# The experts' stage of an attention-and-experts kernel: the order of its operations taken from a written list instead of from a greedy planner

## The chip, the cores and the metric

One core of a Trainium2 chip runs the whole program. The metric is the device time of one execution in microseconds (us), the median of three runs. The core's engines are TensorE (PE, with its weight loads on PEld), VectorE (DVE), ScalarE (ACT), GpSimd (POOL) and the queue SP that only issues transfers. Every engine works through its own instructions strictly in the order of the program and meets the others through semaphores.

## What is computed

The reference first does attention with pooled queries for 64 heads (sequence 1152, head size 64, queries pooled by two) and lays the result out as 4608 tokens of 512 values. Then each token goes to one of eight experts. Tokens are taken greedily by their gate value, and each expert takes 576:

```
logits = x @ w_gate                      # 4608 x 8
for idx in argsort(-logits.flatten()):   # the largest value of all first
    tok, e = idx // 8, idx % 8
    if tok is free and expert e has room: give tok to e
for e in range(8):
    out[tokens of e] = relu(x[tokens of e] @ w1[e]) @ w2[e]    # 512 -> 1024 -> 512
```

## The kernel before

Attention comes first and isn't touched. It leaves the tokens in DRAM (`x_dram`) and the gate values in `L`. The stage that the change touches is `experts` (L1092). It handles the experts one after the other, k = 0 to 7, in the order in which they fill up, and each of them has three parts:

- `route(k)` (L1245) finds the k-th expert and its 576 tokens. For k = 0 to 6 it makes eight rounds: DVE compares keys (`cmp`, L1278), PE counts (`pc`, five small products, L1284), DVE sums its own part (`own`, L1287 and L1289), PE makes the total (`pt`, L1293), DVE narrows the search (`fa`, `fl`). Then come the members (`cl`, `me`), a running sum (`px`, L1362 and L1365), offsets on PE (`pf`, L1370 to L1373), a table lookup on PE (`pl`, L1418), the token numbers on DVE (`ix`, L1422 to L1429), and what is left for the next expert (`tk`, L1466 and L1468; `p9` on PE, L1470; `lf`, `se`). Products `p9`, `pc` and `pt` and what `ix` reads lie in one PSUM tile, `rt`.
- `fetch(k)` (L1555) issues, on POOL's software DMA queue, the load of W1 (`dw`, in two halves for k = 0), the gathers of the tokens in five chunks of up to 128 rows (`dx`, L1564), and the load of W2 (`dv`, L1559). It turns the tokens over (by PE transposes for k below 2, by DVE and SP's queue after that) and splits tokens and weights into a high and a low part: ACT makes the high parts (`xh`, `wh`, `vh`), DVE or POOL the low ones (`xl`, `wl`, `vl`). For k = 0 the first quarter of W1's low part is DVE's (L1633), the rest POOL's (L1634).
- `ffn(k)` (L1639) makes the first layer: for each of 8 blocks of 128 features and each half of the tokens (256 and 320 columns) twelve products (`mm`, L1650), a relu on ACT (`re`, L1655), the low part of the result on DVE (`rs`, L1659 and L1662). Then it makes the second layer: five chunks of tokens, 24 products each or 16 for the last and smaller one (`m2`, L1680 and L1677), an output step on ACT (`ot`; chunk 4 also needs one on DVE, L1690), and a scatter to DRAM on POOL's queue (`pu`, L1697).

Nothing of that is run when it is written down. Each operation is given to `od.add` with its engine, an assumed duration, what it reads and writes, and a tag. `od.emit` (L80 and L1709) then fixes the order in which the program is made, and so the order on every engine. Before, `od` is an `Order` (L51): a greedy planner that follows a clock of assumed durations and, whenever an engine is free, takes of the ready operations the one with the best priority. The priority is the expert's place plus a lead for each tag (`ELEAD`, L1079); `ELATE` (L1085) and the waits in L43 to L48 correct the assumed times at which results are ready. Every single product is an operation of its own there. The small filler products of expert 0's routing (`warm`, L1256) have no tag.

Of the kernel before, what the change touches and what calls it, by code (L numbers as in the profile page):

```python
# [10 lines left out]
def _warn_once_fixed(msg, *args, **kwargs):  # L11
# [31 lines left out]
EOWN = {"PE": 0, "ACT": 140, "DVE": 120, "POOL": 130, "SP": 60}  # L43
EWAIT = {"PE": {"ACT": 205, "DVE": 205, "POOL": 205, "SP": 205},
         "ACT": {"PE": 190, "DVE": 145, "POOL": 170, "SP": 150},
         "DVE": {"PE": 180, "ACT": 130, "POOL": 160, "SP": 150},
         "POOL": {"PE": 130, "ACT": 110, "DVE": 110, "SP": 100},
         "SP": {"PE": 60, "ACT": 60, "DVE": 60, "POOL": 60}}  # L48


class Order:  # L51
# [10 lines left out]
    def __init__(self, lead={}, late={}):  # L62
        self.items, self.lead, self.late = [], lead, late
        self.of, self.cur, self.kind, self.stick, self.early, self.lock = [], None, [], 0, (), []
        self.switch = 83

    def add(self, t, eng, dur, fn, r=(), w=(), late=0, first=0, tag=None, kind=0, lock=None, k=None):

        if self.cur == 0 and tag in self.early:
            first = 1  # L70
        if self.cur == 0 and tag:
            tag = "0" + tag
        late = late + self.late.get(tag, 0)
        pri = t + self.lead.get(tag, 0) + (self.lead.get(f"{tag}.{k}", 0) if k is not None else 0)
        self.items.append((t, len(self.items), eng, dur, fn, tuple(r), tuple(w), late, (-first, pri)))
        self.of.append(self.cur)
        self.kind.append(kind)
        self.lock.append(eng == "POOL" if lock is None else lock)
# [84 lines left out]
class Timed(Order):  # L163
# [21 lines left out]
    def emit(self):  # L185
        items = sorted(range(len(self.items)), key=lambda i: (self.items[i][0], i))
        writer, readers, n = {}, {}, len(items)
        need = [set() for _ in range(n)]
        for i, j in enumerate(items):
            _, _, _, _, _, r, w, _, _ = self.items[j]  # L190
            for k in r:
                if k in writer:
                    need[i].add(writer[k])
                readers.setdefault(k, []).append(i)
            for k in w:
                if k in writer:
                    need[i].add(writer[k])
                need[i].update(readers.get(k, ()))
                readers[k] = []
                writer[k] = i  # L200
            need[i].discard(i)
        users, left = [[] for _ in range(n)], [len(x) for x in need]
        for i, x in enumerate(need):
            for j in x:
                users[j].append(i)
        heap = [(self.when(items[i]), i) for i in range(n) if not left[i]]
        heapq.heapify(heap)
        done = 0
        while heap:
            _, i = heapq.heappop(heap)  # L210
            self.items[items[i]][4]()
            done += 1
            for j in users[i]:
                left[j] -= 1
                if not left[j]:
                    heapq.heappush(heap, (self.when(items[j]), j))
        assert done == n


# [283 lines left out]
def attention(ctx, tc, top, kb, sx, kt, qt, v, wg, x_dram, L, npair=NPAIR):  # L503
# [549 lines left out]
    for n in range(1, npair, 2):  # L1053
# [8 lines left out]
        else:  # L1062
# [13 lines left out]

LT = {"dve": 0, "pe": 0, "x": 8000, "w": 9900, "w0": 3700, "w1": 8000, "x0": 3000, "zd": 0, "kd": 2, "cs": 4, "wn": 4,
      "xm": 7500, "xp": 4}
ELEAD = {"ar": 4.9, "be": 51.6, "bo": 2.8, "cl": 28.5, "cmp": 29.1, "dv": 1.5, "dw": -46.1, "dx": -41.8,  # L1079
# [5 lines left out]
ELATE = {"ar": -300, "bo": -300, "cl": -300, "cmp": 150, "dv": 1900, "dw": 750, "dx": 1500, "fa": -150, "fl": -300,  # L1085
# [4 lines left out]


def experts(ctx, tc, top, kb, sx, x_dram, L, w1, w2, out, C):  # L1092
    nc = tc.nc
    const = ctx.enter_context(tc.tile_pool(name="moe_const", bufs=1))
    psum = ctx.enter_context(tc.tile_pool(name="moe_psum", bufs=1, space=PSUM))
    od = Order(ELEAD, ELATE)
    od.OWN, od.WAIT, od.switch = EOWN, EWAIT, 125
    J = NBLK

    def one(shape, dt, name):  # L1100
# [65 lines left out]
    re = early([128, 1], F32, "re")  # L1166
# [22 lines left out]
    ws = [x.bitcast(F32)[:, 1:2] for x in we]  # L1189
# [12 lines left out]
    rb, tb = rt[:, :128], rt[:, 128:]  # L1202
# [560 lines left out]
```

## Time and profile before

| | us |
|---|---|
| median of 3 runs (1226.16 to 1227.74) | 1226.99 |
| time of the profiled execution | 1229.76 |
| its span, first to last instruction | 1227.9 |

The span is what the trace's clock counts. The execution's own time is 1.86 us more, and it is 2.77 us above the median of the three runs. In the trace the experts' first DVE instruction stands at 751.24 us and PE's last product ends at 1222.13 us. A view of stretches gives the busy time of each engine in it; a row of the timeline gives start, duration, engine, line and operation, and in brackets how long the engine had been idle before it and what released it.

### The profile page before, as it was taken

To read this page: it belongs to the slowest core of one execution; us is meant where nothing else is said; L and a number is where in the kernel's file an instruction comes from. 1 tells how busy PE (TensorE), PEld (TensorE's weight loads), DVE (VectorE), ACT (ScalarE), POOL (GpSimd) and SP (SyncE) were. 2 spreads that over 40 slices of the span, in tenths; PEclk is the share of its full clock that TensorE was granted. 3 is DMA by queue.
4 is the path that set the end of the run, shared out by engine and by line. 5 is a ranking of instruction groups with operands and counts; after the bars stand their busy time and mean duration, and the time that the engine had idled before them with its cause. 6 is when DMAs were issued, how large, how long until landed. Compare 5 with 4: busy or idle time off the path is not lost.

```text
span 1227.9 us, 37291 instructions
## 1 busy us (share of the span) xinstructions
PE 1171.8 (95%) x14875; PEld 806.2 (66%) x14875; DVE 977.8 (80%) x2327; ACT 868.1 (71%) x1603; POOL 897.7 (73%) x913
## 2 busy tenths in 40 slices
PE   7899999999899999999999997799999999999998
PEld 4566666666566666666666665567767777787876
DVE  7999999999999999999999955888988888442120
ACT  6788887987787987887879671376567564766831
POOL 4588888888788888888888882355677746769541
PEclk8899999999999999999999998999999999999999
DMA  8665665675565675666565310514544436345211
GB/s 212 147 172 133 176 168 129 158 182 124 145 176 121 166 179 132 162 169 151 144 177 143 82 48 21 176 35 167 189 153 149 162 124 214 86 168 167 88 40 39
DMA packets 95692, 171.07 MB, mean 139 GB/s; under 512 B 17694, under 2 KB 54558, under 8 KB 93342
## 3 DMA queue, kind: packets, MB, share of 16 engines
q1 hardware_dynamic: 82574, 107.09, 33.1%
q0 software_dynamic: 12800, 61.58, 17.0%
q8 instruction: 117, 1.92, 0.7%
q14 instruction: 57, 0.47, 0.1%
q10 hardware_dynamic: 144, 0.02, 0.0%
HBM read 99.63 MB, written 18.87 MB: 97 GB/s over the span
## 4 chain that ended last, share of the span: by engine, by line
PE 70%; DVE 18%; issue 5%; ACT 2%; DMA 2%; POOL 1%; SPq 0%; POOLq 0%; DVEq 0%; ACTq 0%
PE av L874 13%; PE po L1680 12%; PE ph L1650 12%; DVE MX L741 7%; PE sc L840 6%; PE sc L841 6%; PE mt L748 5%; PE kb L840 3%; PE kb L841 3%; PE av L910 3%; DVE PM L862 1%; PE mt L937 1%; PE rt L1284 1%; DVE V L691 1%; PE po L1677 1%
## 5 line engine op out<-in xcount | busy, mean ns | idle before, releaser
L862 POOL TENSOR_TENSOR PM<-P 128x512 f16<-128x512 f32 x537 | 586.5, 1160 | 116.4 <-ACT P L857 104.3
L741 DVE TENSOR_REDUCE MX<-mt 128x2 f32<-128x1024 f32 (+2 forms) x341 | 374.0, 1130 | 18.7 <-PE mt L748 13.1
L874 PEld LDWEIGHTS <-P 128*128 128x128 bf16 x4608 | 230.0, 98 | 60.0 <-issue 26.3
L857 ACT ACTIVATE P<-sc 128x512 f32<-128x512 f32 x384 | 224.8, 605 | 46.4 <-PE sc L841 41.6
L874 PE MATMUL av<-V,P 128*128 128x65 f16 (+1 forms) x4608 | 243.3, 193 | 0.1
L874 PE MATMUL av<-V,PM 128*128 128x65 f16 x2304 | 235.4, 195 | 0.2 <-POOL PM L862 0.2
L874 PEld LDWEIGHTS <-PM 128*128 128x128 f16 x2304 | 212.2, 97 | 0.5 <-POOL PM L862 0.4
L841 PE MATMUL sc<-QB,KB 66*128 66x64 f16 (+2 forms) x768 | 179.1, 288 | 0.0
L840 PE MATMUL sc<-QA,KA 128*128 128x512 f16 (+1 forms) x768 | 177.7, 288 | 0.8 <-ACT P L857 0.3
L1680 PE MATMUL po<-W2H,HX 128*128 128x512 f32 x512 | 165.7, 398 | 0.0
L857 ACT ACTIVATE P<-kb 128x512 f32<-128x512 f32 x192 | 115.2, 600 | 65.9 <-PE kb L841 63.6
L840 PEld LDWEIGHTS <-KA 128*128 128x128 f16 x1152 | 96.9, 99 | 80.9 <-issue 41.2
L1650 PE MATMUL ph<-Xh,W1h 128*128 128x320 f16 (+1 forms) x512 | 147.0, 287 | 1.5 <-ACT Xh L1512 1.5
L1650 PE MATMUL ph<-Xl,W1h 128*128 128x320 f16 (+1 forms) x512 | 146.8, 287 | 0.6 <-DVE Xl L1514 0.6
L1650 PE MATMUL ph<-Xh,W1l 128*128 128x320 f16 (+1 forms) x512 | 146.9, 287 | 0.0
L1659 DVE SCALAR_TENSOR_TENSOR HX<-ph,HX 128x256 fp32r<-128x256 f32 x128 | 53.3, 417 | 95.4 <-ACT HX L1655 95.2
L1680 PE MATMUL po<-W2L,HX 128*128 128x512 f32 (+1 forms) x320 | 127.4, 398 | 0.0
L841 PEld LDWEIGHTS <-KB 66*128 66x128 f16 (+1 forms) x1152 | 95.3, 98 | 37.5 <-issue 2.7
L1650 PEld LDWEIGHTS <-W1h 128*128 128x128 f16 x1024 | 98.0, 98 | 29.9 <-issue 5.2
L1655 ACT ACTIVATE HX<-ph 128x256 fp32r<-128x256 f32 (+1 forms) x128 | 52.1, 409 | 86.8 <-PE ph L1650 83.3
L1680 PEld LDWEIGHTS po<-W2H,HX 128*128 128x128 f32 x512 | 94.6, 188 | 18.9 <-issue 1.5
L1634 POOL TENSOR_TENSOR W1l<-W,W1h 128x512 f16<-128x512 f32 x62 | 71.6, 1165 | 35.6 <-ACT W1h L1628 30.8
(270 smaller groups left out, 2272.9 us busy)
## 6 DMA issues: line engine op xcount, KB each, us to landing
KD<-in_kt_dram SPq DMA_DIRECT2D x64, 288.0 KB
VD<-in_v_dram SPq DMA_DIRECT2D x32, 576.0 KB
QA<-QH SPq DMA_DIRECT2D x128, 72.0 KB
KA<-KH SPq DMA_DIRECT2D x64, 144.0 KB
KB<-KH SPq DMA_DIRECT2D x64, 144.0 KB
KA<-KL SPq DMA_DIRECT2D x64, 144.0 KB
x_dram<-X SPq DMA_DIRECT2D x16, 576.0 KB
QS<-in_qt_dram SPq DMA_DIRECT2D x31, 288.0 KB
```

Of the source, the lines that this page charges most:

```text
L741: od.add(t, "DVE", d, lambda: nc.vector.tensor_reduce(dst, src, axis=AX.X, op=OP.max), r=[f"m{m}"], w=w, tag="mr", k=z)
L748: nc.tensor.matmul(mt[s][:, y], pairs[b][s], KH[i][h, ks], start=True, stop=True)
L840: nc.tensor.matmul(c, KA[i][:, s, ks], QA[i][:, s, qs], start=first, stop=False, skip_group_check=True)
L841: nc.tensor.matmul(c, KB[i][:kr, s, ks], QB[i][:kr, s, qs], start=False, stop=last, skip_group_check=True)
L857: od.add(g + 0.1, "ACT", 480, lambda: nc.scalar.activation(p, c, AF.Exp, scale=1.0 / UNIT), r=[ck], w=[("P32", g % NP)], tag="exp", k=g % ...
L862: od.add(g + 0.2, en, dur, lock=1, fn=lambda: eng.tensor_tensor(pm, p, hi, op=OP.subtract), r=[("P32", g % NP)], w=[("PM", g % NM)], tag=" ...
L874: nc.tensor.matmul(out, w[:, qs], v, start=kb == 0 and j == 0 and y == 0, stop=kb == NKB - 1 and y == 2, skip_group_check=True)
L1634: eng.tensor_tensor(o, a, b, op=OP.subtract), r=[key] + sr + [(nm + "H", z, y)], w=[(nm + "L", z, y)], first=first, lock=1, tag="wl" if nm ...
L1650: nc.tensor.matmul(p, a[:, d, fs], b[:, d, qs], start=z == 0, stop=z == 11)
L1655: nc.scalar.activation(HH[:, f, qs], p, AF.Relu)
L1659: V.scalar_tensor_tensor(HL[:, f, 64 + 256 * hf:320 + 256 * hf], p[:, :256], 0.0, h[:, :256], op0=OP.max, op1=OP.subtract)
L1680: nc.tensor.matmul(o[:n], a[:, z, q0:q0 + n], b[:, z], start=z == 0 and y == 0, stop=z == 7, skip_group_check=True)
```

## The change

A new class `Listed` takes the place of `Order` in `experts`. It puts the operations of a tag of one expert together in the order in which they were added: four `mm` products make one group, two `m2` products make one, everything else stands alone. Each group has a name (expert, tag, running number; operations without a tag get the engine's name, so the fillers are `pe_`) and a number in the table `ETIME`, 2503 of them, given in ns from the start of the stage. `emit` makes the groups in the order of these numbers, except that a group waits its turn until all groups that it depends on are made. The durations, leads and late times are not used any more. No operation is added, removed or given to another engine; the operands are the same, and attention is the same.

```
+
+class Listed(Order):
+
+    def __init__(self, table):
+        Order.__init__(self)
+        self.table, self.names = table, []
+
+    def add(self, t, eng, dur, fn, r=(), w=(), late=0, first=0, tag=None, kind=0, lock=None, k=None):
+        Order.add(self, t, eng, dur, fn, r, w, late, first, tag, kind, lock, k)
+        self.names.append((int(t // 10), tag or {"PE": "pe", "DVE": "dv", "POOL": "po", "ACT": "ac", "SP": "sp"}[eng] + "_"))
+
+    def emit(self):
+        group, made, seen = {}, [], {}
+        for i in sorted(range(len(self.items)), key=lambda i: (self.items[i][0], i)):
+            k, tag = self.names[i]
+            z = seen[k, tag] = seen.get((k, tag), -1) + 1
+            name = f"{k}{tag}{z // {'mm': 4, 'm2': 2}.get(tag, 1)}"
+            if name not in group:
+                group[name] = len(made)
+                made.append((name, [], [], []))
+            _, fns, r, w = made[group[name]]
+            fns.append(self.items[i][4])
+            r.extend(x for x in self.items[i][5] if x not in r)
+            w.extend(x for x in self.items[i][6] if x not in w)
+        n, writer, readers = len(made), {}, {}
+        need = [set() for _ in range(n)]
+        for i, (_, _, r, w) in enumerate(made):
+            for k in r:
+                if k in writer:
+                    need[i].add(writer[k])
+                readers.setdefault(k, []).append(i)
+            for k in w:
+                if k in writer:
+                    need[i].add(writer[k])
+                need[i].update(readers.get(k, ()))
+                readers[k] = []
+                writer[k] = i
+            need[i].discard(i)
+        users, left = [[] for _ in range(n)], [len(x) for x in need]
+        for i, x in enumerate(need):
+            for j in x:
+                users[j].append(i)
+        heap = [(self.table[made[i][0]], i) for i in range(n) if not left[i]]
+        heapq.heapify(heap)
+        done = 0
+        while heap:
+            _, i = heapq.heappop(heap)
+            for fn in made[i][1]:
+                fn()
+            done += 1
+            for j in users[i]:
+                left[j] -= 1
+                if not left[j]:
+                    heapq.heappush(heap, (self.table[made[j][0]], j))
         assert done == n
...
-ELEAD = {"ar": 4.9, "be": 51.6, "bo": 2.8, "cl": 28.5, "cmp": 29.1, "dv": 1.5, "dw": -46.1, "dx": -41.8,
...
+ETIME = {"0be0": 0, "0be1": 580, "0be2": 1100, "0be3": 1620, "0ke0": 490, "0ke1": 950, "0ke2": 1470, "0ke3": 1990,
+         ...
+         "0ke8": 40973, "0ke9": 38213, "0po_0": 26276, "0dx0": 30168, "0dx1": 31468, "0dx2": 33186, "0dx3": 34582,
+         "0dx4": 35882, "0po_1": 37182, "0dv0": 40836, "0tr0": 34150, "0tr1": 34368, "0xh0": 34791, "0xl0": 35573,
+         ...
+         "0ws1": 34959, "0ws2": 48224, "0ws3": 48968, "0wi0": 40803, "0wi1": 49258, "0wh0": 35271, "0wl0": 36173,
+         "0wh1": 35786, "0wl1": 36863, "0wh2": 36781, "0wl2": 38282, "0wh3": 38341, "0wl3": 39591, "0wh4": 49268,
+         ...
+         "0vh0": 50526, "0vl0": 51776, "0vh1": 51606, "0vl1": 53021, "0vh2": 55796, "0vl2": 57094, "0vh3": 57956,
+         ...
+         75211, "0pu0": 75861, "0m212": 53151, "0m213": 54975, "0m214": 56047, "0m215": 71249, "0m216": 75006,
+         ...
+         74870, "1st2": 74135, "1st3": 72665, "1pl0": 76368, "1ix0": 78235, "1sh0": 69818, "1tk1": 79771, "1p90":
+         82910, "1lf0": 83154, "1se0": 80826, "1be0": 75605, "1be1": 76095, "1be2": 76675, "1be3": 77195, "1be4":
+         ...
+         "7m243": 462358, "7m244": 462812, "7m245": 463266, "7m246": 463720, "7m247": 464174, "7ot3": 464833, "7pu3":
+         465483, "7m248": 455548, "7m249": 456002, "7m250": 456456, "7m251": 456910, "7m252": 457364, "7m253":
+         457818, "7m254": 458272, "7m255": 458726, "7ot4": 459385, "7ot5": 460010, "7pu4": 460770}
...
 def experts(ctx, tc, top, kb, sx, x_dram, L, w1, w2, out, C):
...
-    od = Order(ELEAD, ELATE)
-    od.OWN, od.WAIT, od.switch = EOWN, EWAIT, 125
+    od = Listed(ETIME)
```

Places in the list that the prediction speaks of, in its own numbers:

- Expert 0, ACT: `xh0`, `wh0`, `wh1`, `xh1`, `wh2`, `xh2`, `wh3`. DVE: `ws1`, `xl0`, `wl0`, `wl1`, `xl1` with small steps between. POOL: `dx0` to `dx4`, the load of W1's second half (`po_1`), `wl2`, `wl3`, and then the load of W2 (`dv0`). PE: the first `m2` group (`0m212`) comes behind 24 `mm` groups and needs `vh0` and `vl0`.
- `p9` and `ix`: for k = 1 the list has `pl0` at 76368, `ix0` at 78235, `tk1` at 79771 and `p90` at 82910, with 26 second-layer products between `pl0` and `p90`. For k = 2 to 5 there are 40 first-layer and 10 second-layer products, 24 first-layer ones, 10 second-layer ones and 24 second-layer ones. In each case `ix0` and `tk1` stand ahead of `p90`.
- `px`: for k = 1 and 2 no `rs` stands between `cl0` and `px0`.
- In 17 of the 48 rounds of experts 1 to 6, one `rs` or more stands on DVE between `cmp` and `own`.
- The last chunk of expert 7's second layer is chunk 3 (`7ot3`, `7pu3`); chunk 4 (`7ot4`, `7ot5`, `7pu4`) comes before it. Before, the chunks went out in the order 0 to 4.

## Rows read from the trace of the kernel before

**Rows 1.** Busy time by stretch: start, length, each engine's busy us, PE clock, DMA.

```profile
791.20:796.00 4.80, 4.16 (x22) 2.85 (x22) 4.66 (x15) 3.14 (x6) 1.80 (x2) 0.64 1.02 413
796.00:1030.00 234.00, 226.28 (x1706) 168.76 (x1704) 203.56 (x858) 148.29 (x278) 156.88 (x161) 1.00 0.43 143
1030.00:1222.20 192.20, 192.13 (x1230) 152.98 (x1228) 57.99 (x202) 107.91 (x206) 111.74 (x127) 1.00 0.35 112
```

**Rows 2.** Waits of PE from 796 us on: total us, times, longest.

```profile
PE rt L1470 <- DVE idx L1429: 2.9, 3, 1.5
PE rt L1293 <- DVE red L1289: 2.0, 2, 1.4
PE rt L1370 <- DVE tot L1365: 1.8, 2, 1.3
PE rt L1284 <- DVE GE L1278: 0.8, 3, 0.3
```

**Rows 3.** Timeline of PE, expert 0's first products of the first layer.

```profile
791.25 0.27 PE L1650 MATMUL ph<-Xh,W1h 128*128 128x256 f16 x1 [1.48 <-ACT Xh L1512]
792.11 0.27 PE L1650 MATMUL ph<-Xl,W1h 128*128 128x256 f16 x1 [0.59 <-DVE Xl L1514]
...
796.55 0.27 PE L1650 MATMUL ph<-Xh,W1l 128*128 128x256 f16 x1
796.66 0.30 PE L1650 MATMUL ph<-Xh,W1h 128*128 128x320 f16 x1
796.79 0.30 PE L1650 MATMUL ph<-Xl,W1h 128*128 128x320 f16 x1
```

**Rows 4.** Timeline of ACT ahead of expert 0's first product.

```profile
787.43 1.33 ACT L1626 ACTIVATE W1h<-W,we 128x512 f16<-128x512 f32 x2 [0.63 <-DVE we L1597]
...
789.24 0.71 ACT L1624 ACTIVATE W<-W,we 128x512 f32<-128x512 f32 x1
789.99 0.62 ACT L1628 CAST W1h<-W 128x512 f16<-128x512 f32 x1
790.51 0.68 ACT L1512 ACTIVATE Xh<-po,sx 128x512 f16<-128x512 f32 x1
```

**Rows 5.** Timeline of DVE in the same stretch.

```profile
788.36 1.42 DVE L1633 SCALAR_TENSOR_TENSOR W1l<-W,we,W1h 128x512 f16<-128x512 f32 x2
789.70 0.74 DVE L1514 SCALAR_TENSOR_TENSOR Xl<-po,sx,Xh 128x512 f16<-128x512 f32 x1
...
791.31 0.74 DVE L1514 SCALAR_TENSOR_TENSOR Xl<-po,sx,Xh 128x512 f16<-128x512 f32 x1
```

**Rows 6.** All token gathers, L1564: us from issue to landing.

```profile
DMA to landing us min/median/max: 2.9/3.5/5.2
```

**Rows 7.** Timeline of POOL: expert 0's W2 load, its second subtraction from W1.

```profile
788.39 0.94 POOL L1559 DMA_INDIRECT W<-in_w_dram,widx  x1 [0.30 <-issue]
...
792.53 1.15 POOL L1634 TENSOR_TENSOR W1l<-W,W1h 128x512 f16<-128x512 f32 x1 [0.69 <-ACT W1h L1628]
```

**Rows 8.** All 17 weight loads, L1559: us from issue to landing.

```profile
DMA to landing us min/median/max: 5.7/10.0/12.3
```

**Rows 9.** Timeline of DVE inside expert 1's routing: one `rs`.

```profile
824.24 0.41 DVE L1659 SCALAR_TENSOR_TENSOR HX<-ph,HX 128x256 fp32r<-128x256 f32 x1
824.58 0.21 DVE L1662 SCALAR_TENSOR_TENSOR HX<-ph,HX 128x64 fp32r<-128x64 f32 x1
```

**Rows 10.** Timeline of PE: second-layer products with a `pc` between them.

```profile
892.68 0.39 PE L1680 MATMUL po<-W2H,HX 128*128 128x512 f32 x1
892.91 0.40 PE L1680 MATMUL po<-W2L,HX 128*128 128x512 f32 x1
...
893.34 0.71 PE L1680 MATMUL po<-W2H,HX 128*128 128x512 f32 x2
893.88 0.40 PE L1680 MATMUL po<-W2L,HX 128*128 128x512 f32 x1
```

**Rows 11.** Timeline of DVE behind the last product.

```profile
1222.89 0.74 DVE L1690 SCALAR_TENSOR_TENSOR OT<-po,wf,O 64x512 f32<-64x512 f32 x1 [25.18 <-ACT O L1688]
```

More of the change, by code (lines that the diff above doesn't have):

```diff
@@ L216, in emit @@
                     heapq.heappush(heap, (self.when(items[j]), j))
+        assert done == n
+class Listed(Order):
[48 more added lines that the diff above has]
+                    heapq.heappush(heap, (self.table[made[j][0]], j))
         assert done == n
@@ L1078 @@
       "xm": 7500, "xp": 4}
-ELEAD = {"ar": 4.9, "be": 51.6, "bo": 2.8, "cl": 28.5, "cmp": 29.1, "dv": 1.5, "dw": -46.1, "dx": -41.8,
[5 rows of a table removed]
-ELATE = {"ar": -300, "bo": -300, "cl": -300, "cmp": 150, "dv": 1900, "dw": 750, "dx": 1500, "fa": -150, "fl": -300,
[4 rows of a table removed]
+ETIME = {"0be0": 0, "0be1": 580, "0be2": 1100, "0be3": 1620, "0ke0": 490, "0ke1": 950, "0ke2": 1470, "0ke3": 1990,
[386 rows of a table added]
 def experts(ctx, tc, top, kb, sx, x_dram, L, w1, w2, out, C):
```

384 rows, old and new, of tables (ELATE, ELEAD, ETIME) are left out of this document.

## The prediction

> **What bounds the kernel now.** I read three views in this order. First the stretches of the experts' stage: from 796 to 1030 us PE is busy for 226.28 of 234.00 us and DVE for 203.56, so PE sets the pace there and DVE, at 87%, is close behind; from 1030 to 1222.2 us PE has 192.13 of 192.20 us [rows 1]. The products are the same before and after, so all that another order can win is PE's idle time, what goes on before the first product, and what follows the last. Second, the waits of PE: from 796 us on they add up to 2.9 + 2.0 + 1.8 + 0.8 = 7.5 us in ten waits, all of them small routing products that wait for DVE [rows 2]. The difference of the busy time, 7.7 us, says the same. After 1030 us there is nothing to win. Third, the timeline at expert 0's first product: PE is idle for 1.48 us until ACT has made the high part of the second chunk of tokens, and for 0.59 us more until DVE has made its low part [rows 3]. That much is the ceiling; the list moves some two thousand operations to win a few microseconds of it.
>
> I read the order out of the list and take no time from its numbers; all durations below are the trace's.
>
> **Step 1: the start of expert 0's first layer.** Before, ACT does W1h twice (1.33 us from 787.43), the first chunk's Xh, another quarter of W1 (scale and cast, 789.24 to 790.51) and only then the second chunk's Xh, which ends at 791.19 [rows 4]; the product at 791.25 starts right behind it. In the list the first Xh stands ahead of W1h, where ACT is idle for 0.63 us before 787.43 (0.68 long, so W1h starts some 0.1 late), and the second Xh comes straight behind W1h: 787.5 + 1.33 + 0.68 = 789.5. On DVE before, W1l twice (1.42) is followed by the first Xl at 789.70, routing steps, and the second Xl from 791.31 to 792.05 [rows 5]. In the list the first Xl comes before W1l: 787.6 + 0.74 = 788.3, W1l twice until 789.75 and the second Xl until 790.5. The product that started at 792.11 can start at about 790.5. I take **1.6 us gained**. The bounds are 0 (if the first chunk's tokens land no earlier than W1) and 1.6 plus a slower clock that ends: between 791.2 and 796 the granted clock averages 0.64, a mixture of 1.2 and 2.4 GHz behind a stretch in which PE had mostly waited, and 36% of 4.8 us is 1.7 us [rows 1]. I don't count on that part, since PE waits ahead of this point in the new order too.
>
> The tokens come by five gathers which POOL issues while DVE writes its comparison steps; in the trace a gather lands 2.9 to 5.2 us after its issue, median 3.5 [rows 6], and I leave that as it is. The Trainium skill ("SBUF — State Buffer", the section "A bandwidth-pool intuition that's wrong (but worth ruling out)") says that a DMA issued from GpSimd is held until a DVE instruction that uses both ports has ended, 3100 ns in place of 620. By that rule the gathers, which now meet other DVE work, could each lose 2.48 us, an estimate from that page, and if the one that the first product waits for did, the sum would be 3.3 us in place of 5.8 and the time 1223.7; a spread of 2.3 us over forty gathers under a busy DVE does not show a loss of that kind as the usual case, nor does it exclude one.
>
> **Step 2: the waits after 796 us.** `p9` waits 2.9 us in three places for `idx` [rows 2], the end of the long index step, because it writes the tile that this step reads. The list puts `ix` and `tk` ahead of `p9` and for every k at least ten second-layer or 24 first-layer products between the lookup and `p9`. Ten at 0.23 us [rows 10] are 2.3 us, as long as the longest of these waits and more. I count all 2.9 us as gained. `pf` waits 1.8 us for the running sum; in the longer case DVE had put an `rs` of 0.41 + 0.21 us between the members and that sum [rows 9]. In the list none stands there for k = 1 and 2: gained, 1.8. `pt` (2.0 us) and `pc` (0.8) wait for the steps of a round. The list still has an `rs` inside 17 of 48 rounds; I let half of the first and all of the second stay. **Gained: 2.9 + 1.8 + 1.0 = 5.7 us**, 1.8 stays. Bounds 0 and 7.5.
>
> **Step 3: W2 of expert 0.** This is where the list costs something. Before, POOL issues this load at 788.39. In the list it stands behind the subtractions `wl2` and `wl3`, which need ACT's `wh2` and `wh3`. From step 1: Xh ends at 789.5, `wh2` 1.27 later (789.24 to 790.51 [rows 4]), another Xh 0.68, `wh3` 1.27, the subtraction 1.15 [rows 7], 0.3 for POOL to go on: the issue is at about 794.2, 5.8 us later. Loads land 10.0 us after their issue in the median [rows 8]: 804.2. ACT's cast (0.62) and POOL's subtraction (1.15) make it 806.0. PE gets to its first second-layer product behind 24 groups: 48 products at 0.11 and 48 at 0.13 us [rows 3], 11.5 us, and I estimate 1.8 us for the transposes and three rounds in between, so 790.5 + 13.3 = 803.8. PE waits **2.2 us lost**. W1's second half is issued before W2 in both orders, so it doesn't move. Bounds: 0, since the fastest load took 5.7 us (it is a half-sized one), and 4.5 with the slowest, 12.3. Behind this product on PE stands a round of expert 1, so DVE waits too; the later W2 loads are listed a whole layer of products ahead of their use.
>
> **Step 4: turns between the layers.** When PE comes back to second-layer products from a `pc`, the next two take 893.88 - 893.34 = 0.54 us where two take 0.46 (892.91 - 892.68 is 0.23) [rows 10], so each turn costs 0.08 us besides the small products. The list turns to the second layer 68 times. I cost the difference at nothing, bounds 1 us either way (twelve turns more or fewer). SP's queue gets the same moves for k of 2 and above, later than their tokens by the same steps; they are hidden by a whole expert's products, 50 us, and would cost PE directly without that cover.
>
> **Step 5: the end.** Before, the last chunk is the small one, which needs an ACT and then a DVE step of 0.74 us [rows 11]. In the list it is chunk 3, with the ACT step alone. **Gained: 0.7 us**; the scatter and its landing stay.
>
> **Sum.** 1.6 + 5.7 - 2.2 + 0.7 = 5.8 us. Against the profiled execution's own 1229.76 us this is 1223.96; that execution is 2.77 us above the median, and the same gain from 1226.99 is 1221.2 us.
>
> **Rivals.**
>
> *The waits move on instead of going.* PE is in order: each of the 96 `pc` and `pt` of experts 1 to 6 holds everything behind it, and in place of the ten waits other ones of the same sum come up. For it: DVE is 87% busy, and only a few products stand between steps. Against it: the places named in step 2 are clear mistakes of the old order. Then 1.6 - 2.2 + 0.7 is 0.1 us: 1226.9.
>
> *DVE falls behind and the kernel gets slower.* The place is the round of experts 1 to 6, between `cmp` and `own`. Where an `rs` stands there, `own` waits for a relu that waits for first-layer products, and `pt` waits for `own`. If in all 17 such rounds PE waited for the whole `rs`, 0.62 us [rows 9], that is 10.5 us, and the sum is -4.7: 1231.7. It decides from 8.3 us on, 0.5 us in each of these rounds. Against it: the old order had such waits at `pt` only twice.
>
> *The order on the chip hardly differs.* The list gives way to dependences, and PE was full anyway: 1227.0. The places of `p9` and the last chunk speak against it.
>
> **How the numbers follow.** Forecast as summed: 0.70, by itself 1217 to 1225. Waits move on: 0.12. DVE falls behind: 0.12. Hardly differs: 0.06. A measurement of this kernel can tell about 0.2%, 2.45 us, from no change. Nearly all of the forecast and a quarter of the second case are faster, 0.71; the rest of the second, the last case and small parts of the others are the same, 0.16; slower is 0.13. With every bound at its best the gain is 1.6 + 1.7 + 7.5 + 0.7 + 1.0 = 12.5 us, 1214.5; with every one at its worst -4.5 - 1.0 + 0.7 = -4.8, 1231.8. Eight in ten lie between 1215 and 1227, since the third case and the far ends are left out.
>
> **What would show it.** Step 1: the first product with Xl about 39.3 us after 751.24, the experts' first DVE instruction, in place of 40.9. Step 2: no wait of L1470 for `idx` in the waits of PE, and L1370 under 0.3 us. Step 3: a PE wait at the first second-layer product of expert 0, with W2L on POOL as its releaser, and the W2 load issued behind two subtractions. Step 5: no DVE step behind the last product. The prediction is wrong if PE's waits after the start come to 7 us or more, or if the gaps at `pc` and `pt` grow.

## The result, and the profile after

The changed kernel takes 1235.6 us (median of 7 runs, 1231.44 to 1236.48); the kernel before takes 1227.74 in the same comparison (7 runs, 1226.16 to 1230.68). The ratio is 1.0051, 95% interval 1.0034 to 1.0068: slower, where I had forecast 1221.2. The profiled execution took 1236.21 us, its span is 1234.4, the experts' first DVE instruction stands at 750.85 and the last product ends at 1229.3.

The stretches of the experts' stage, to be held against [rows 1], and smaller ones where the trouble is (start and end, length, busy us of each engine, PE clock, DMA share, GB/s):

```profile
791.20:796.00 4.80, 3.95 (x34) 3.01 (x33) 4.13 (x15) 2.29 (x6) 2.21 (x3) 1.00 0.84 261
796.00:1030.00 234.00, 223.37 (x1628) 164.82 (x1626) 201.33 (x828) 144.62 (x269) 151.25 (x158) 0.98 0.44 147
1030.00:1222.20 192.20, 191.72 (x1258) 151.92 (x1257) 64.51 (x233) 112.22 (x213) 116.17 (x129) 1.00 0.34 112
...
955.00:960.00 5.00, 4.79 (x38) 3.63 (x34) 4.76 (x25) 1.61 (x3) 2.96 (x4) 1.00 0.98 366
...
960.00:970.00 10.00, 6.09 (x34) 3.44 (x32) 3.80 (x20) 6.36 (x12) 4.24 (x4) 0.84 0.25 60
970.00:980.00 10.00, 9.93 (x78) 7.17 (x78) 7.73 (x26) 7.39 (x15) 9.02 (x10) 0.82 0.41 131
980.00:990.00 10.00, 7.22 (x53) 5.23 (x51) 8.21 (x17) 3.94 (x9) 6.72 (x9) 0.83 0.16 48
```

From 796 to 1030 PE is idle for 10.6 us where it was for 7.7, and its clock is 0.98 of full instead of 1.00. Of the 10.6 us 6.8 lie between 960 and 990, and so does the slower clock. Below are PE's waits from 796 us on (total, times, longest), against [rows 2]:

```profile
PE ph L2081 <- DVE HX L2090: 2.9, 2, 2.8
PE ph L2081 <- ACT Xh L1976: 2.9, 1, 2.9
PE po L2111 <- ACT OT L2116: 1.8, 3, 0.9
PE rt L1724 <- DVE red L1720: 1.0, 2, 0.6
PE ph L2081 <- POOL Xl L1980: 1.0, 1, 1.0
PE rt L1901 <- DVE idx L1860: 0.2, 1, 0.2
```

The waits of `p9` (2.9 us, now L1901) and `pf` (1.8) have all but gone, as step 2 said. Three new ones of 2.9, 1.0 and 2.8 us stand at first-layer products; all three are expert 3's.

To see when time is won and lost I counted PE's work done by a moment: every product at its spacing at full clock, 0.109 or 0.136 us in the first layer [rows 3], 0.227 in the second [rows 10], some 0.03 for a small product of the routing, from the experts' first DVE instruction on. The **lead** is that count minus the one of the kernel before at the same moment:

| us into the experts' stage | 60 | 120 | 180 | 210 | 220 | 230 | 240 | 260 | 460 |
|---|---|---|---|---|---|---|---|---|---|
| lead of the kernel after, us | 2.2 | 6.0 | 5.9 | 4.7 | -0.9 | -2.6 | -6.7 | -6.5 | -7.3 |

For 210 us the forecast is right in kind: 4.7 against 1.6 + 5.7 - 2.2 = 5.1 without the end. That the size fits so well is in part luck, since single terms are off in both directions (see below). Then 11.4 us are lost within 30. The timeline there, by engine (SP, POOL, ACT, DVE, PE), and the landing of the load that POOL issues at 952.06:

```profile
946.13 11.23 SPq L1962 DMA_DIRECT2D XG<-XB  x16
...
952.06 0.97 POOL L1990 DMA_INDIRECT W<-in_w_dram,widx  x1 [0.30 <-issue]
...
965.03 2.43 POOL L1980 TENSOR_TENSOR Xl<-XG,Xh 128x512 f16<-128x512 f32 x2 [6.96 <-ACT Xh L1976]
...
976.10 7.39 POOL L2065 TENSOR_TENSOR W2L<-W,W2H 128x512 fp32r<-128x512 f32 x6
...
955.82 0.82 ACT L1976 CAST Xh<-XG 128x512 f16<-128x512 f32 x2
963.58 0.72 ACT L1974 ACTIVATE XG<-XG,sx 128x512 f32<-128x512 f32 x1 [6.94 <-DMA XG<-XB]
...
979.87 3.64 DVE L2033 TENSOR_TENSOR wf<-we,sx 128x1 f32<-128x1 f32 x1
983.43 0.41 DVE L2090 SCALAR_TENSOR_TENSOR HX<-ph,HX 128x256 fp32r<-128x256 f32 x1
...
963.09 0.32 PE L1715 MATMUL rt<-W,GE 128*128 128x64 bf16 x5
966.28 0.27 PE L2081 MATMUL ph<-Xh,W1h 128*128 128x256 f16 x1 [2.87 <-ACT Xh L1976]
967.51 0.37 PE L2081 MATMUL ph<-Xl,W1h 128*128 128x256 f16 x1 [0.96 <-POOL Xl L1980]
...
983.90 0.37 PE L2081 MATMUL ph<-Xh,W1h 128*128 128x256 f16 x1 [2.78 <-DVE HX L2090]
...
DMA to landing us min/median/max: 10.7/10.7/10.7
```

**First hole.** SP issues the 16 moves that turn expert 3's tokens over from 946.13 to 957.36. In the midst of them, at 952.06, POOL issues the 2 MB load of expert 4's W1. It fills the transfers (DMA share 0.98 from 955 to 960) and lands 10.7 us later, at 962.8. ACT, which scales what the moves bring, waits 6.94 us and goes on at 963.58; PE waits behind it for 2.87 us and behind POOL's low part for 0.96.

**Second hole.** The step `wf` on DVE, which multiplies two columns of 128x1, takes 3.64 us; of its nine executions the median is 0.16. It begins in the fourth of POOL's six back-to-back subtractions of 128x512 (sums, in what follows) and ends with the last of them (976.10 + 7.39 = 983.49). The next relu rest (`rs`) stands behind it on DVE, and PE waits 2.78 us for that.

**The clock.** From 960 to 990 PE is granted 0.84, 0.82 and 0.83 of full, a mixture of 1.2 and 2.4 GHz behind its idling, where the rest from 796 to 1030 shows 1.00. 10 x (0.16 + 0.18 + 0.17) is 5.1 us, an upper bound, since PE did not work all through. With 2.9 + 1.0 + 2.8 us of waits that makes at most 11.8, against 11.4 lost.

In the kernel before the same moves had far more room, by its timeline of SP, ACT and PE:

```profile
934.64 12.11 SPq L1531 DMA_DIRECT2D XG<-XB  x16
...
952.41 0.71 ACT L1543 ACTIVATE XG<-XG,sx 128x512 f32<-128x512 f32 x1
...
968.99 0.28 PE L1650 MATMUL ph<-Xh,W1h 128*128 128x256 f16 x1
```

There the products of expert 3 began 34.4 us after the first move, and the load was issued at 951.21, behind the last move. In the kernel after PE was ready at 963.4, 17.3 us after the first move.

### The profile page after: what moved, and what is told of

Its sections match the earlier page's. It is cut to its first block, busy times and chain, and to the rows that moved or that the text cites. A ratio compares the mean times of both kernels' runs of the same rounds, so it can differ in the third digit from the quotient of the medians.

```text
span 1234.4 us, 37218 instructions
## 1 busy us (share of the span) xinstructions
PE 1177.8 (95%) x14875; PEld 809.1 (66%) x14875; DVE 982.4 (80%) x2327; ACT 869.4 (70%) x1603; POOL 897.0 (73%) x913
## 3 DMA queue, kind: packets, MB, share of 16 engines
q0 software_dynamic: 12800, 61.58, 17.1%
## 4 chain that ended last, share of the span: by engine, by line
PE 59%; DVE 20%; ACT 7%; issue 6%; DMA 3%; POOL 2%; SPq 1%; POOLq 0%; ACTq 0%; DVEq 0%
PE av L930 13%; PE ph L2081 8%; PE po L2111 7%; DVE MX L797 7%; PE sc L896 6%; PE sc L897 6%; PE mt L804 5%; PE kb L896 3%; PE kb L897 3%; PE av L966 3%; ACT W L2055 2%; ACT W1h L2059 2%; DVE PM L918 1%; DVE V L747 1%; PE mt L993 1%
## 5 line engine op out<-in xcount | busy, mean ns | idle before, releaser
L2111 PE MATMUL po<-W2H,HX 128*128 128x512 f32 x512 | 168.4, 400 | 2.0 <-ACT OT L2116 1.8
L2081 PE MATMUL ph<-Xh,W1h 128*128 128x320 f16 (+1 forms) x512 | 144.4, 289 | 6.9 <-DVE HX L2090 2.9
L2081 PE MATMUL ph<-Xh,W1l 128*128 128x256 f16 (+1 forms) x512 | 142.9, 289 | 0.0
```

Source lines behind the costliest of these rows:

```text
L2081: nc.tensor.matmul(p, a[:, d, fs], b[:, d, qs], start=z == 0, stop=z == 11)
L2111: nc.tensor.matmul(o[:n], a[:, z, q0:q0 + n], b[:, z], start=z == 0 and y == 0, stop=z == 7, skip_group_check=True)
```

## The experiments

Each ratio is to runs of the kernel before on the same chip. The edits are to `ETIME` (list times in ns), except where code is shown. Leads are read as above.

**E1: the load later**, with the scales and casts that hang on it, past the moves and ahead of expert 4's gathers (`4dx0` at 208360).

```diff
+ETIME.update({"4dw0": 207900, "4wq0": 217700, "4wq3": 219900, "4wq2": 221600, "4wq1": 222700, "4ws0": 225000,
+    "4ws1": 225300, "4wi0": 225320, "4wh1": 226100, "4wl1": 228000, "4wh2": 227700, "4wl2": 229300})
```

> The changed kernel, with one thing moved in the list: the load of expert 4's W1 (and the steps that use it) stands behind expert 3's low token parts, so that it is issued after the 16 moves of expert 3's tokens have landed. Theory 1 (the load of 2 MB shares the DMA engines with the moves, and makes the last of them land at 963.5, some 6.5 us late): ACT no longer waits 6.9 us for them, PE's waits of 2.9 for Xh and 1.0 for Xl at expert 3's first product go to under 1 us together, and the time falls by 4 to 6 us, to 1230 to 1231.5, since the low clock behind that wait goes too. Rival (expert 3's products are simply listed ahead of what DVE and the queue can do): ACT's wait stays at over 5 us, and the time within 1 us of 1235.6, or above.

1230.64 us (1227.6 to 1237.22), ratio 1.0017 (1.0002 to 1.0031). PE's waits for Xh and for POOL's Xl are gone, and ACT waits 0.5 us for the moves in place of 6.94:

```profile
ACT XG L1976 <- DMA XG<-XB: 0.5, 1, 0.5
```

From the first move to expert 3's first product there are 17.1 us, as in the kernel after. So the load made the first hole, and that much time is enough without it. The edit also moves `wf` (`4wi0`, 218697 in the list): it begins where POOL is idle and takes 0.16 us, so the second hole is gone too. But the lead still falls, to 1.9 at 220 and -1.0 at 240: one new wait of 3.9 us, for DVE's HX. That the time lies in the expected range is luck, then: one hole stands in place of another.

**E2: the step `wf` later.**

```diff
+ETIME.update({"4wi0": 240000})
```

> The changed kernel, with the last small DVE step of expert 4's weight scale (the one that took 3.64 us at 979.87 in place of 0.16, until POOL's row of six subtractions ended) put some 20 us later in the list, where its result is still early. Theory 2 (this step was held by POOL's work, and with it the relu's rest behind it and PE for 2.8 us): PE's wait of 2.8 us for HX goes, and the time falls by 2.5 to 4 us, to about 1232. Rival (DVE was late for another reason, or the next two-operand step is held in its place): PE's wait stays, the time within 1 us of 1235.6. The first hole, at 963 to 968 us, stays in both.

1231.75 us (1229.36 to 1235.27), ratio 1.0032 (1.0019 to 1.0044). The wait for HX falls from 2.8 to 0.2 us, the lead at 240 is -2.4 in place of -6.7, and the first hole stays (Xh 3.7 us). At its new place `wf` is held again, for 1.16 us, and PE waits 1.0 us behind it for the routing's table.

**E3: both** edits together.

> Both moves together. If the two holes are all that the change lost, as the progress of PE says (5 us ahead of the kernel before at 210 us of the stage, 6 us behind at 240), the time is 1227.7 less 4 to 6: 1222 to 1224, faster than the kernel before. If theory 1 is wrong, it is that of the run with the later small step; if PE's lead is lost in later stages anyway, 1226 to 1229.

1231.29 us (1226.46 to 1234.17), ratio 1.0022 (1.0009 to 1.0036): a miss of some 8 us. The trace says where it went. Below are POOL, DVE and PE, and the gathers' time from issue to landing:

```profile
961.65 0.98 POOL L1992 DMA_INDIRECT W<-in_w_dram,widx  x1
962.94 0.96 POOL L1997 DMA_INDIRECT XG<-x_dram,idx  x1 [0.31 <-issue]
...
971.02 0.71 DVE L1957 STREAM_TRANSPOSE XB<-XG 128x512 f32<-128x512 f32 x1 [3.77 <-DMA XG<-x_dram,idx]
...
971.97 0.21 DVE L2095 SCALAR_TENSOR_TENSOR HX<-ph,HX 128x64 fp32r<-128x64 f32 x1
...
972.23 0.31 PE L2083 MATMUL ph<-Xh,W1h 128*128 128x320 f16 x1 [3.55 <-DVE HX L2095]
...
DMA to landing us min/median/max: 6.0/7.1/8.1
```

The load now stands just ahead of expert 4's five gathers on the same software queue. They land 6.0 to 8.1 us after their issue, where all forty before took 2.9 to 5.2 [rows 6]. DVE waits 3.77 us with a transpose for the first of them, the relu rests stand behind it, and PE waits 3.55. The edit had moved the collision, not removed it. And nothing more was to be had from `wf`: E1 had already taken it out of POOL's way, and here, at 240 us of list time, it is held for 1.11 us.

**E4: filler products** in the first hole of the kernel after, to ask what the clock costs: 24 products of 288 columns ahead of expert 3's first layer, their results unused.

```diff
+ETIME.update({f"3pe_{z}": 209050 for z in range(24)})
 def ffn(k, t):
     i = k
+    for z in range(24 if k == 3 else 0):
+        od.add(t + 0.49, "PE", 122, lambda: nc.tensor.matmul(ph[0][0][:, :J * E], ones, e8.rearrange("p j e -> p (j e)"),
+            start=True, stop=True), w=[("ph", 0, 0)], kind=1)
```

> The changed kernel with 24 filler products of 288 columns (some 2.9 us of PE's time) ahead of expert 3's first product, where PE waited for 3.8 us in two steps. What it adds: products whose results nothing reads. Theory (the wait also costs because the granted clock falls to 0.68 and 0.64 between 965 and 975 us): the fillers fit into the wait, the clock stays at 1.0 there, and the time falls by 1 to 3 us. Rival (the low clock costs nothing, as PE waits for others in that stretch): the time stays within 0.7 us. If the fillers do not fit, it is up to 2.9 us longer.

1235.09 us (1232.19 to 1238.79), ratio 1.0064 (1.0045 to 1.0084): no gain, a miss. The clock from 970 to 990 is 1.00 with them, but the lead at 240 is -6.0 against -6.7: the fillers take nearly what they give back, and the hold of `wf` was longer (4.55 us). What the clock costs apart from the waits is read from the stretches above and not shown by a run.

**E5: the load behind the gathers**, with its scales and casts 4 us later; `wf` stays at 240 us.

```diff
+ETIME.update({"4dw0": 214500, "4wq0": 222200, "4wq3": 224200, "4wq2": 226100, "4wq1": 227600, "4ws0": 229500,
+    "4ws1": 229800, "4wi0": 240000, "4wh1": 230300, "4wh2": 231400, "4wh5": 232500, "4wh4": 233400, "4wh3": 234300,
+    "4wl1": 232000, "4wl2": 233300, "4wl5": 234300, "4wl4": 235500, "4wl3": 236700})
```

> The kernel after with expert 4's W1 load listed behind expert 4's five token gathers (it stood ahead of the 16 moves' end, then, in the runs with the load later, just ahead of the gathers), its scale and casts some 4 us of list time later than there, and the write-weight step at 240 us of list time. Theory A (the 2 MB load holds up whatever small transfer is issued just behind or beside it, first expert 3's moves, then expert 4's gathers, whose 3.8 us wait on the first transpose stopped the rest step HX and with it PE for 3.5 us): the 3.5 us wait goes, TensorE's lead over the kernel before at 240 us into the experts is 4 to 5 us instead of 1.3, and the time is 1223 to 1226, ratio to the kernel before 0.995 to 0.998. Theory B (there is always a next wait; the list has no slack there): PE waits at some other producer for 2 us and more between 960 and 990, and the time stays 1228 to 1231, ratio 1.001 to 1.003.

1249.88 us, ratio 1.0039 (1.0021 to 1.0058), on a chip where the kernel before takes 1245.6. Its trace has waits that no earlier one has, of 2.8 and 3.6 us at the small routing products during runs of gathers; `wf` is held there for 4.90 us, and PE waits 6.4 us for the table behind it. With the unnamed waits in it, this run does not decide between the theories.

**E6: a probe** of the held step. It computes nothing of the kernel (zeros go to the first 128 rows); 48 sums on POOL run beside sixty groups of four steps on DVE.

```diff
+for r in range(6):
+    for j in range(8):
+        nc.gpsimd.tensor_tensor(Lo[:, j], A[:, j], H.bitcast(F32)[:, j], op=OP.subtract)
+for r in range(60):
+    nc.vector.tensor_scalar(c[:, 0:1], a[:, 0:1], 2.0, 1.0, op0=OP.mult, op1=OP.add)
+    nc.vector.tensor_scalar(c[:, 1:2], c[:, 0:1], 2.0, 1.0, op0=OP.mult, op1=OP.add)
+    nc.vector.tensor_tensor(c[:, 2:3], c[:, 1:2], b[:, 0:1], op=OP.mult)
+    nc.vector.tensor_reduce(c[:, 3:4], b[:, 0:32 + r % 32], axis=AX.X, op=OP.max)
```

> A probe that leaves out everything of the computation (it writes zeros to the first 128 rows): 48 GpSimd sums of two 128x512 tensors back to back, beside 60 groups on VectorE of two one-operand steps, one 128x1 step with two operands in SBUF and one reduction. Theory H (a two-operand VectorE step whose start falls into GpSimd's work can be held until GpSimd pauses, over several instructions): some of the 60 two-operand steps take 1 us and more, up to many times one GpSimd step, while the others and all one-operand steps take their usual 0.1 to 0.2 us. Rival (the 3.64 us of the write-weight step had another cause, such as a semaphore or the clock): all 60 take under 0.6 us, as 0.42 was in the kernel before.

Groups of instructions of the probe (line, engine, operation, count | busy us, mean ns), and the two-operand step by itself (min/median/max ns):

```profile
L63 POOL TENSOR_TENSOR Lo<-A,H 128x512 fp32r<-128x512 f32 x48 | 58.6, 1255 | 5.4 <-ACT H L60 5.4
L66 DVE TENSOR_SCALAR c<-c 128x1 f32<-128x1 f32 x60 | 9.2, 153 | 1.0
...
L67 DVE TENSOR_TENSOR c<-c,b x60: 159/903/1077, 6.1 to 69.7; 128x1 f32<-128x1 f32 x60
```

48 of the sixty two-operand steps begin while POOL works. Each of them lasts until the sum into which it falls has ended, 0.91 us in the mean; the other twelve, behind POOL's last sum, take 0.16. The one-operand steps are never held. That a step is held over several sums, as in the kernel after, did not come up in the 48. But the probe locks the two engines together, so that nearly all of its steps begin at the same point, some 0.35 us into a sum.

**E7 to E10: the two kernels, E3 and E5 again**, on one chip.

> The kernel before, unchanged, traced again beside the next three on one chip, because the previous comparison ran 1.5 per cent slower on both sides (1245.6 us for the kernel before), with waits named remote that no earlier trace has. If the chip is what differs: its time is that of the kernel before in the same call, and where that is again near 1245 its trace shows the same unnamed waits of VectorE, 5 us and more in sum between 900 and 1030. If the unnamed waits came from the edit of the run with the load behind the gathers: none here.

> The kernel after, unchanged, on the same chip as the three beside it. Ratio to the kernel before 1.004 to 1.007 as in the first comparison, if the two holes (moves behind the load, write-weight step held) are of the program; if they hang on one chip's timing, 0.998 to 1.002.

> The run with the load and the write-weight step later, again, on the same chip: ratio to the kernel before 1.001 to 1.004, with the 3.5 us wait for HX behind the first transpose, which waits for gathers queued behind the 2 MB load.

> The run with the load behind the gathers, again, on the same chip as the others. Theory A (the load on the software queue holds up what is issued behind it): 2.5 to 4 us less than the run beside it with the load ahead of the gathers, ratio to the kernel before 0.995 to 0.999, no wait of PE over 2 us between 960 and 985. Theory B (always a next wait): within 1 us of that run, ratio 1.001 to 1.004, and PE waits 2 us and more at another producer there.

The kernel before: 1228.57 us, 0.999 (0.9974 to 1.0006) of its other runs there, with none of the unnamed waits; so this chip is not of E5's kind. The kernel after: 1.0054 (1.0032 to 1.0076), the same two holes in its trace and a lead of -6.8 at 240. E3: 1.0008 (0.9989 to 1.0026). E5: 1233.36 us, 1.0028 (1.0011 to 1.0045), against theory A by the time. Its trace says something else (POOL, DVE, PE, and the gathers' landing):

```profile
993.94 5.27 POOL L1982 TENSOR_TENSOR Xl<-XG,Xh 128x512 f16<-128x512 f32 x6
999.17 1.14 POOL L2067 TENSOR_TENSOR W1l<-W,W1h 128x512 f16<-128x512 f32 x1
...
995.44 4.89 DVE L2035 TENSOR_TENSOR wf<-we,sx 128x1 f32<-128x1 f32 x1
...
1001.99 0.32 PE L1851 MATMUL rt<-TAB,ST 128*128 128x38 f16 x5 [6.41 <-DVE TAB L1812]
...
DMA to landing us min/median/max: 3.2/3.8/4.0
```

The gathers land in 3.2 to 4.0 us again, PE has no wait above 1 us from 945 to 995, and the lead at 240 is 4.9. Then `wf`, which I had pushed to 240 us of list time myself, falls into POOL's next run of sums, is held for 4.89 us, and PE loses 8.2 (lead -3.3 at 260).

**E11 and E12: `wf` alone**, on top of E5: E11 by its place, E12 by its form. **E13** is the kernel after with E12's form and nothing moved.

```diff
+ETIME["4wi0"] = 229820                     # E11
...
-V.tensor_tensor(wf[k][:, h:h + 1], we[h].bitcast(F32)[:, 2:3], xi, op=OP.mult)
+V.tensor_scalar(wf[k][:, h:h + 1], we[h].bitcast(F32)[:, 2:3], xi[:, 0:1], None, op0=OP.mult)
```

> The run with the load behind the gathers, with one place changed: the write-weight step of expert 4 is listed right behind the step whose result it takes (229.8 us of list time instead of 240), where GpSimd was idle from 979.3 to 984.3 in that run; at 240 it began at 995.4, 1.5 us into seven back-to-back GpSimd sums, took 4.9 us and PE stood for 6.4 us behind it. Theory (all three waits between 210 and 260 are placing: moves against the load, gathers against the load, the step against GpSimd's run): the step takes 0.16 us, PE waits nowhere over 1.2 us after 960, the lead over the kernel before at 260 is 4 to 5 us instead of -3.3, and the time is 1224 to 1226, ratio 0.995 to 0.998. Rival (there is always a next wait): another wait of 2 us and more before 280, ratio 1.000 to 1.003.

> The run with the load behind the gathers, its write-weight step still at 240 us of list time, but written with its second factor as a per-partition scalar, so that it has one operand of 128x1 and not two. Theory (VectorE's step with two float32 operands in SBUF is what GpSimd's run holds): it takes 0.15 to 0.2 us beside GpSimd's sums, all of its like in the run too, the 6.4 us wait of PE goes, lead at 260 of 4 to 5 us, ratio 0.995 to 0.998. Rival (any step at this place is held, or the reading of the product's other inputs is): it takes 3 us and more again, ratio 1.002 to 1.004.

> The kernel after with nothing moved, only the write-weight step of all experts with its second factor as a per-partition scalar. Theory: the 3.6 us step goes, the wait for HX of 2.8 us with it, the moves' hole stays: lead at 240 of about -2.4 us instead of -6.7, as in the run with the step listed later, and ratio 1.002 to 1.004 instead of 1.0054. Rival (the step's length is of its place): 1.0045 to 1.0065.

| run | median us | ratio to before | interval | lead at 240 | 260 | 460 |
|---|---|---|---|---|---|---|
| E11 | 1226.74 | 0.9981 | 0.9967 to 0.9994 | 4.6 | 2.4 | 2.0 |
| E12 | 1227.08 | 0.9977 | 0.9961 to 0.9993 | 4.9 | 2.4 | 2.0 |
| E13 | 1231.33 | 1.0018 | 1.0003 to 1.0032 | -2.8 | -2.7 | -3.4 |

E11 and E12 beat both kernels. From E12 (DVE and PE):

```profile
997.28 0.21 DVE L2035 TENSOR_SCALAR wf<-we,sx 128x1 f32<-128x1 f32 x1
...
999.14 0.28 PE L1851 MATMUL rt<-TAB,ST 128*128 128x38 f16 x5 [1.73 <-DVE TAB L1812]
```

At the very place where the two-operand form took 4.89 us the other takes 0.21. In E13 the form alone is worth some 1.0054 - 1.0018 = 0.36%, 4.4 us (E8 and E13 ran on different chips, and their intervals meet at 1.0032), where the second hole's wait of 2.8 us and the clock from 980 to 990, 10 x 0.17, make 4.5 at most: the lead at 240 is -2.8 in place of -6.7. E11's and E12's expectations for the lead at 260 were 2 us too high; PE still waits 1.4 or 1.7 us there for the table.

**E14 to E16: relief for ACT**, on top of E12, twice, the second time beside E12 itself.

```diff
+ETIME.update({"4wh4": 240050, "4wh3": 240450, "4wl4": 242300, "4wl3": 243600})
```

> The run with the one-operand step and the load behind the gathers, with two of ACT's quarters of W1 of expert 4 (scale and cast, 1.34 us each) and GpSimd's subtractions of them listed behind the four token chunks instead of ahead. In that run the lead fell from 4.9 to 2.7 us between 240 and 250: ACT was 98 per cent busy from 990 to 1000, VectorE waited 1.4 us there for its relu, and PE 1.73 us for the table that follows. Theory (my own shift of the scales and casts made that wait): it falls under 0.6 us, the lead at 260 is 4 to 5 us and at 460 3.5 to 4.5, ratio 0.995 to 0.998. Rival (the table's step is late whatever ACT does): PE still waits 1.4 us or more there, ratio as before, 0.997 to 0.999.

> The run with ACT relieved, again, beside the run that it was made from: its last comparison fell on a chip where the kernel before took 1242.6 us and where its trace has unnamed waits of 2.7 to 3.7 us of all engines during the gathers. On a chip where the kernel before takes 1227 to 1230: lead at 260 of 4 to 5 us, at 460 3.5 to 4.5, ratio 0.995 to 0.998, 1 to 2 us under the run beside it. On a chip of the other sort: as far under the run beside it, both near a ratio of 1. If the table's step is late whatever ACT does: within 0.7 us of the run beside it.

> The run with the one-operand step, unchanged, as the control of the run beside it on the same chip: ratio 0.996 to 0.999 on a chip where the kernel before takes 1227 to 1230, as the last time (0.9977).

E14 fell on a chip where the kernel before takes 1242.56 us: 1242.16, ratio 1.0003 (0.9986 to 1.0019). Waits of its other engines that have no releaser in the trace:

```profile
DVE dg L1720 <- remote: 11.7, 4, 3.7
ACT HX L2088 <- remote: 5.3, 2, 4.2
ACT OT L2119 <- remote: 3.0, 1, 3.0
```

E15 on an ordinary chip: 1226.5 us, 0.9975 (0.9957 to 0.9994); E16, the control: 1227.2, 0.9975 (0.9958 to 0.9992). PE's waits in E15:

```profile
PE po L2113 <- ACT OT L2118: 3.1, 5, 1.2
PE rt L1726 <- DVE red L1722: 1.0, 2, 0.6
PE rt L1851 <- DVE TAB L1812: 0.3, 1, 0.3
```

The wait for the table falls to 0.3 us (1.7 in E12, 1.8 in the control), and 1.2 us of it come back at once as a wait for ACT's output step. The lead at 260 is 2.9 against 2.2 in the control, where 4 to 5 were expected, and the times do not differ beyond their noise. So the cause of the wait was named rightly, but the next wait took its place. Where the last 2 us between 240 and 250 are to be had stays open.

## Why the prediction was wrong

**Step 1 held.** The first product with Xl stands at 790.10, 39.25 us after the first DVE instruction, where 39.3 was forecast. The part that I had not counted on came too: the granted clock from 791.2 to 796 is 1.00 in place of 0.64, and the lead at 60 is 2.2 us for 1.6.

**Step 2 held, a little short.** Without the three new waits PE's waits from 796 us on are 3.1 us against 7.5: 4.4 gained of 5.7, since 1.8 us of waits for ACT's output step are new. With the three they come to 9.8 us, over the 7 that I had named as a sign of being wrong.

**Step 3 was mis-sized**: 2.2 us forecast as lost, 0.4 measured. The load was issued at 793.21 (794.2 worked out), behind two subtractions as I had said, and landed in 8.6 us in place of the median 10.0, at 801.8. W2's low part was ready at 805.7, close to the 806.0 worked out, and PE's weight load waited for it as I had said:

```profile
PEld po L2111 <- POOL W2L L2065: 0.4, 1, 0.4
```

What was off is PE's own way there: it came to its first second-layer product at 805.2, not at 803.8, because the estimate of 1.8 us for transposes and rounds left out waits of its own, 0.85 us at 794.12 for another chunk's Xl and 0.62 at 804.34 for a round's sum.

**Step 4 failed**, in the sentence that SP's moves "are hidden by a whole expert's products, 50 us, and would cost PE directly without that cover". The second half was right. The first was assumed: the cover was 34.4 us before and 17.3 us after, both readable ahead of the run, one from the timeline, the other from the list, where the load of expert 4 (199172) stands among the moves of expert 3 (192450 to 202200), which end 7 us of list time ahead of the products that need them (209194). I had read the list for PE, DVE and POOL and only said of SP's queue that it gets "the same moves". E1 shows the load as the cause: with the same 17 us of cover and the load out of the way, PE did not wait. So what the step left out is the other transfer beside the moves, more than the cover's length. It cost 3.8 us of waits and the slower clock behind them.

**No step had the second hole.** In the kernel before, `wf` of expert 4 began among POOL's sums too, but was held for 0.42 us only, to the end of one short sum (DVE and POOL):

```profile
998.85 0.42 DVE L1602 TENSOR_TENSOR wf<-we,sx 128x1 f32<-128x1 f32 x1
...
996.13 5.51 POOL L1549 TENSOR_TENSOR Xl<-XG,Xh 128x512 f16<-128x512 f32 x6 [16.01 <-ACT Xh L1545]
```

In the list it fell into another run of six and was held for 3.64 us, ahead of a relu rest that PE needed. I had weighed a rule on holds between DVE and POOL for the gathers and did not look for DVE's own steps under it. The Trainium skill ("SBUF — State Buffer", the section "SBUF: two separate sides") says that a VectorE step with two inputs in SBUF and a GpSimd step that reads SBUF exclude each other, and that whichever starts first has the ports for its whole instruction. The probe agrees for one step (up to 1.08 us). The kernels differ from it in both directions: `wf` is held over several sums, and other steps with two operands are not held at all, see the last section.

**Step 5 held**: from the last product to the end of the span 5.1 us in place of 5.8, with no DVE step behind it.

**The rivals.** "DVE falls behind" comes near the measured time with the wrong mechanism: PE waited for a round's sum only twice, 1.0 us in all, and the planner's order had an `rs` inside about as many rounds, 18 in place of 17. "The waits move on" had the kind right and the price wrong. It assumed as much to come back as goes; three waits of one expert, with the clock behind them, took back twice that. E11, E12, E15 and E16 show that it need not be so: with the load behind the gathers and `wf` listed elsewhere (E11) or written in the other form (the others), the list is 0.2% faster than the planner (0.9975 to 0.9981).

## What to carry to other kernels

When an order is changed, every queue's turn against every other's has to be read, and above all which small transfers with a deadline a large load is issued next to: here a 2 MB load cost whatever stood beside or behind it, first SP's moves, then its own queue's gathers, until it was issued last. A tiny step in front of a critical one on an in-order engine deserves a look at what it shares with other engines: writing its second factor as a per-partition scalar was worth some 4 us. And where an experiment removed a wait and did not win the time (E1, E3, E5), it had set up the next wait itself; the trace of the experiment names it.

## What the runs showed of the hardware

- A DVE step with two operands of 128x1 float32 in SBUF that begins inside a run of POOL's sums is held, at times to the end of one sum (0.41 to 1.16 us) and at times to the end of the whole run, over three to five sums: 3.64 us in the kernel after and 3.61 in its repeat, 4.55 in E4, 4.90 and 4.89 in the two runs of E5. What decides between the two is open; the probe has only the first kind. Other two-operand steps of that stage are not held: in E5's second run 13 of the 28 comparisons below began inside a sum of POOL's, and all took the same time (min/median/max ns).

```profile
L1846 DVE TENSOR_TENSOR ST<-slots,kb x28: 806/814/822, 823.3 to 1097.6; 128x640 f16<-128x640 f16 x28
```

- Gathers issued right behind a 2 MB load on the software queue land in 6.0 to 8.5 us (E1, E3) instead of 3.2 to 4.0 (E5 again), and moves of 64 and 80 KB on SP's queue beside it kept ACT waiting until 0.8 us after the load had landed.
- On two of the chips the kernel before took 1242.6 and 1245.6 us, over 1% more than on the others. In the traces of E5 and E14 there several engines stop together for some 3 us during runs of gathers, with no releaser named; the longest such waits are 3.7 us of DVE and 4.4 of ACT. Of the kernel before there is no trace on these chips, and the cause is open.
